# Attention, a channel mix and a routed expert layer in one kernel: how the dispatch builds its index tables, and where three small slots stand

## The chip, the cores and the metric

The kernel runs as one program on one core of a Trainium2 chip. The metric is the time of one execution on the device in microseconds, the median of three runs; lower is better. A profile comes from one further execution. Engines: TensorE (PE), VectorE (DVE), ScalarE (ACT), GpSimd (POOL) and SyncE (SP), which issues most DMAs.

## The reference

Three layers follow one another; batch 4, 576 tokens each, width 512.

```python
# 1: attention, 8 heads of 64, masked by blocks of 64
scores = where(block_i >= block_j, q @ k.T / 8, -1e9); x = softmax(scores) @ v
# 2: a mix of each token with the one before it
xk = mu_k * x + (1 - mu_k) * x_prev;  xr = mu_r * x + (1 - mu_r) * x_prev
x = sigmoid(xr @ w_r) * (relu(xk @ w_k) ** 2 @ w_v)
# 3: each token takes its own best of 8 experts, or the expert of the token before it
fresh = argmax(x @ w_gate);  e = fresh if s == 0 or local_gate[s] < 0.5 else prev_e
out = softmax(x @ w_gate)[e] * (relu(x @ w1[e]) @ w2[e])
```

## The kernel before, in words

The 2304 tokens are 18 tiles of 128 and 9 groups of 256. Attention goes head by head, the mix group by group; products that need precision are made of a high and a low half in a reduced type (a "split"), three matmuls for one. After each group the routing finds the expert of each token, its probability (p_all) and its rank among the tokens of its expert so far (rank_all, `route_group`, L898 to L985).

The expert layer works in slots: one slot holds 128 tokens of one expert. It gathers their rows of y_dram (L1227), loads w1 and w2 of the expert if it is a new one (SyncE, L1256), splits them on ScalarE and VectorE, multiplies twice, scales by the probability and scatters the rows to the output (L1236). 19 main slots run always, six more only if they are needed. Three small slots of at most 32 rows each take the remainders of some experts (`small_slot`, L1326); they keep their weights in four buffers of 256 KB, two of which are the wraw buffers, and load them in four batches one after the other. `BEFORE` (L35) says before which main slots they stand in the program: 10, 13 and 15.

`dispatch` (L1010) makes the tables of the slots: which token is in which place (gidx, sidx) and with which probability (pslot). It runs twice: early after group 6, for the first 14 tiles and the slots 0 to 6, while group 7 and 8 are still mixed; and late after group 8, for all 18 tiles and the other slots. Each time it works out the first place of each expert, from it the place of each token, splits the place into slot (place over 128) and partition (place modulo 128), and turns the list around with TensorE (L1125 to L1133): for each tile a one-hot [128 x 128] of the partition (d_lh), a one-hot of the slot (d_sel) and its product with three values of each token (d_rhs), summed over the tiles into a PSUM bank, pinv, which is copied to d_inv. pinv, the flips of y and the logits of the routing share two banks (`aux`, L776; in the profile they are named s and av).

The order on each engine is written by a planner (`schedule`, L93). It gives each operation a priority by the longest way from it to the end, and all that is not of the rank "ffn" comes ahead of the slots by a large constant (L265 to L267). Then it runs through a model of time: whenever an engine is free, the most urgent operation that is ready by the model is put next. VectorE operations on SBUF and GpSimd's arithmetic are kept apart by it (`turn`). On the chip each engine executes its list in that order and waits at each operation until its inputs are there. Nearly all operations are issued by one line, so the profile calls them L273.

Of the kernel before, what the change touches and what calls it, by code (L numbers as in the profile page):

```python
# [23 lines left out]
NT = T // 128  # L24
GT = 256
# [4 lines left out]
EARLY = -(-(EG * GT - 127 * NE) // 128)  # L30
# [1 line left out]


SMALLS, ROWS = 3, 32
BEFORE = (EARLY + 3, EARLY + 6, EARLY + 8)  # L35
SCALE = 0.125
MASK = -1.0e30

# [5 lines left out]
def f(ap):  # L44
    return ap.bitcast(F32)
# [37 lines left out]

OVER = 65.0

BEGIN = {"pe": 950.0, "act": 1960.0, "dve": 850.0, "pool": 850.0, "sp": 650.0}


# [4 lines left out]
def schedule(ops, until=-1, fill=0.0):  # L93
# [3 lines left out]
    n = len(ops)  # L97
# [20 lines left out]
    while left:  # L118
# [10 lines left out]
        a, b = now[e]  # L129
        if b and turn[other[e]] > t:  # L130

            if not a:
                free[e] = min([turn[other[e]]] + [x[0] for x in soon[e][:1]])
                continue
            i = heapq.heappop(a)[1]
        else:
            i = heapq.heappop(b if b and (not a or b[0] < a[0]) else a)[1]
        start[i] = t
        order.append(i)
        left -= 1  # L140
# [35 lines left out]
class Plan:  # L176
# [87 lines left out]
    def issue(self):  # L264
        ops = self.ops  # L265
        until = next(i for i, o in enumerate(ops) if o[0] == "pe" and o[3][0].tensor.name == self.bank)
        start, order = schedule([(o[0], o[5], o[6], o[8], o[9], o[7][0] != "ffn") for o in ops], until if self.warm else -1, 54.0)  # L267
# [9 lines left out]
def fused_kernel(ctx: ExitStack, tc: tile.TileContext, a, out):  # L277
# [82 lines left out]
    def buffers(where, name, shape=None, dtype=F32, n=1):  # L360
        if name not in rings:
            rings[name] = [0] + [where.tile(shape, dtype, name=f"{name}_{i}") for i in range(n)]
        return rings[name]

    def ring(*args):

        r = buffers(*args)
        r[0] += 1
        return r[1 + (r[0] - 1) % (len(r) - 1)]

    def flat(x):
        return x.rearrange("p a b -> p (a b)")
# [525 lines left out]
    def route_group(g, lg, after):  # L898
# [30 lines left out]
        def to_row():  # L929
            v["pk"] = aux()  # L930
            for j in range(2):
                pe.transpose(v["pk"][0:1, j * 128:j * 128 + 128], v["key"][:, j:j + 1], ident)
            scan = ring(rt, "scan", [1, GT], F32, 1)
# [72 lines left out]
    vals = rt.tile([128, NT, 3], F32, name="vals")  # L1006
    es = rt.tile([1, SLOTS + 1], F32, name="es")
    dve.memset(es[:, 0:1], -1.0)

    def dispatch(early):  # L1010

# [1 line left out]


        st = 0 if early else 1
        nt, j0, n = (EG * 2, 0, EARLY) if early else (NT, EARLY, SLOTS - EARLY)
        m = n if early else n + SMALLS
        gidx_s, sidx_s, pslot_s = of_small()
# [1 line left out]

        def small(name, shape, dt=F32):
            return ring(rt, "d_" + name, shape, dt, 1)

        pc = aux()
        sob = small("sob", [128, NE], BF16)
# [74 lines left out]
        if not early:  # L1100
# [8 lines left out]
        posi = small("posi", [128, 2, NT], I32)[:, :, 0:nt]  # L1109
        dve.tensor_tensor(posi[:, 0, :], posf, rank, op=ALU.add)  # L1110
        dve.tensor_scalar(posi[:, 1, :], posi[:, 0, :], 7, None, op0=ALU.logical_shift_right)
        dve.tensor_scalar(posi[:, 0, :], posi[:, 0, :], 127, None, op0=ALU.bitwise_and)
        pmd = small("pmd", [128, 2, NT])[:, :, 0:nt]
        dve.tensor_copy(pmd, posi)


        ts = slice(0, nt) if early else slice(EG * 2, NT)
        phr = small("phr", [128, NT], F32R)[:, ts]
        dve.tensor_copy(phr, p_all[:, ts])
        dve.tensor_scalar(vals[:, ts, 0], tok[:, ts], 1.0, None, op0=ALU.add)  # L1120
        dve.tensor_copy(vals[:, ts, 1], f(phr))
        dve.tensor_tensor(vals[:, ts, 2], p_all[:, ts], f(phr), op=ALU.subtract)
        w = m + m % 2
        pinv = aux()
        for t in range(nt):  # L1125
# [8 lines left out]
        inv = small("inv", [128, 66])[:, 0:3 * w].rearrange("p (k w) -> p k w", k=3)  # L1134
        dve.tensor_copy(inv, pinv[:, 0:3 * w].rearrange("p (k w) -> p k w", k=3))
        dve.tensor_scalar(sidx[st], inv[:, 0, 0:n], -1.0, None, op0=ALU.add)
        dve.tensor_scalar(gidx[st], inv[:, 0, 0:n], -1.0, 0.0, op0=ALU.add, op1=ALU.max)
        dve.tensor_tensor(pslot[st], inv[:, 1, 0:n], inv[:, 2, 0:n], op=ALU.add)
        if not early:

            dve.tensor_scalar(gidx_s, inv[:, 0, n:m], -1.0, 0.0, op0=ALU.add, op1=ALU.max)
            lh = ring(rt, "d_lh", [128, 128], F32R, 2)
# [3 lines left out]
            pe.matmul(pr[:, 0:3 * SMALLS], f(lh), inv[:, :, n:m], start=True, stop=True)  # L1146
            dve.tensor_scalar(sidx_s, pr[:, 0:SMALLS], 4.0, quarter, op0=ALU.mult, op1=ALU.add)
            dve.tensor_copy(inv[:, 0, 0:SMALLS], pr[:, SMALLS:2 * SMALLS])
            dve.tensor_tensor(pslot_s, inv[:, 0, 0:SMALLS], pr[:, 2 * SMALLS:3 * SMALLS], op=ALU.add)


    def units():
# [287 lines left out]
```

## Time and profile before

| | |
|---|---|
| median of 3 runs | 810.71 us (809.32 to 812.0) |
| the profiled execution | 808.18 us |
| its span, first to last instruction | 806.4 us |
| TensorE busy | 778.0 us, 96% of the span |
| VectorE, ScalarE, GpSimd busy | 609.6, 535.3 and 299.9 us |
| mean granted clock of TensorE | 0.988 of full |
| read from and written to HBM | 131.68 and 9.90 MB |

Times in the views count from the first instruction of the span. The attention and the mix fill the span up to about 524 us, the early dispatch lies at about 477 to 504 us, the late one at 543 to 594 us, and the slots run from 525 us to the end. A busy share is the share of a stretch in which an engine works on an instruction; the durations of neighbours overlap a little, so the distance from start to start is the better price of one operation in a row of such. An idle time names what ended it: "<-DVE d_rhs" means that the engine stood still until VectorE had written d_rhs.

### The profile page before, as it was taken

The page shows a single profiled execution, that of the slowest core. Times are in us where ns is not written, and L with a number is a line of the kernel's source. Part 1 is how long each engine was busy: PE and PEld are TensorE (multiplying, and loading weights), DVE is VectorE, ACT ScalarE, POOL GpSimd, SP SyncE. Part 2 cuts the span into 40 slices and gives each one's busy share as a digit, 9 for nine tenths or more (in the row PEclk, how much of TensorE's full clock was granted, in tenths as well). Part 3 has the DMA queues.
Part 4 walks back from the last instruction along what each step waited for, and adds up shares of the span by engine and source line. Part 5 has one row for each costly group of instructions (what it writes and reads, how often), then busy time and mean ns, then how long its engine had stood idle before and what let it go on. Part 6 is the DMA issues. An engine that isn't in the chain of part 4 may idle for free.

```text
span 806.4 us, 15002 instructions
## 1 busy us (share of the span) xinstructions
PE 778.0 (96%) x5040; PEld 640.3 (79%) x5040; DVE 609.6 (76%) x1346; ACT 535.3 (66%) x1156; POOL 299.9 (37%) x275
## 2 busy tenths in 40 slices
PE   8999999999999999999999997999989999999994
PEld 8665798988888989898998986767867777767773
DVE  6986767775789869576785479699999986866840
ACT  3888566983578946265893525469769977867841
POOL 3343585533656427345452332222121521312200
PEclk9999999999999999999999999899999999999998
DMA  8574312211233202201310005111475287695300
GB/s 216 161 211 153 106 57 82 88 45 35 77 92 99 72 17 83 76 28 37 99 45 14 14 27 209 40 39 40 144 248 197 66 275 268 213 327 187 120 15 23
DMA packets 40466, 87.62 MB, mean 109 GB/s; under 512 B 6540, under 2 KB 10640, under 8 KB 40384
## 3 DMA queue, kind: packets, MB, share of 16 engines
q1 hardware_dynamic: 37152, 76.71, 29.6%
q0 software_dynamic: 3232, 9.90, 3.5%
q8 instruction: 41, 0.67, 0.4%
q14 instruction: 41, 0.34, 0.1%
HBM read 131.68 MB, written 9.90 MB: 176 GB/s over the span
## 4 chain that ended last, share of the span: by engine, by line
PE 67%; issue 11%; DVE 11%; DMA 6%; ACT 2%; POOL 1%; SPq 1%; POOLq 0%; ACTq 0%; DVEq 0%
PE acc L273 38%; PE s L273 12%; PE psT L273 9%; PE av L273 6%; DMA out<-xm,sidx 2%; PE acc L1379 1%; DVE wvl L273 1%; DVE attr L273 1%; DVE xm L273 1%; DMA out<-v,ssum 1%; DVE wrl L273 1%; DMA wraw<-in_w 1%; DMA x<-in_w 1%; ACT attr L273 1%; DVE relu L273 1%
## 5 line engine op out<-in xcount | busy, mean ns | idle before, releaser
L273 DVE TENSOR_REDUCE nm<-s 128x1 f32<-128x576 f32 (+4 forms) x132 | 67.7, 547 | 24.2 <-ACT s L273 22.9
L273 PE MATMUL acc<-xh,wkh 128*128 128x256 f32 x288 | 82.1, 295 | 0.9 <-ACT xh L273 0.6
L273 PE MATMUL acc<-xl,wkh 128*128 128x256 f32 x288 | 82.0, 293 | 0.1
L1236 POOL DMA_INDIRECT out<-xm,sidx x19 | 26.3, 1383 | 147.6 <-ACT xm L273 124.9
L273 PE MATMUL acc<-xh,wkl 128*128 128x256 f32 x288 | 80.7, 289 | 0.0
L273 POOL TENSOR_TENSOR attr<-qk,attr 64x512 fp32r<-64x512 f32 (+1 forms) x48 | 65.7, 1368 | 37.8 <-ACT attr L273 30.3
L273 PE MATMUL av<-attr 128*128 128x256 f32 (+3 forms) x336 | 77.4, 288 | 0.8 <-ACT x L273 0.3
L273 DVE TENSOR_TENSOR attr<-psT,attr 64x256 fp32r<-64x256 f32 (+2 forms) x120 | 63.1, 526 | 17.1 <-ACT attr L273 14.7
L273 POOL TENSOR_TENSOR kkl<-relu,kkh 128x512 fp32r<-128x512 f32 x36 | 47.7, 1329 | 61.9 <-ACT kkh L273 53.6
L273 PE MATMUL s<-attr 128*128 128x288 f32 (+3 forms) x288 | 67.1, 300 | 0.6 <-ACT ea L273 0.6
L273 POOL TENSOR_TENSOR xl<-xm,xh 128x512 fp32r<-128x512 f32 x36 | 46.8, 1301 | 49.7 <-ACT xh L273 45.9
L273 ACT ACTIVATE attr<-psT 64x256 fp32r<-64x256 f32 (+2 forms) x120 | 53.0, 463 | 10.4 <-PE psT L273 9.5
L273 PE MATMUL acc<-attr,wrh 128*128 128x512 f32 x160 | 56.7, 405 | 1.1 <-ACT wrh L273 1.1
L273 ACT ACTIVATE xh<-xm 128x512 fp32r<-128x512 f32 x36 | 22.7, 631 | 52.0 <-DVE xm L273 51.9
L273 PE MATMUL acc<-wvh,kkh 128*128 128x512 f32 x144 | 56.6, 414 | 0.0
L273 PEld LDWEIGHTS acc<-xh,wkh 128*128 128x128 f32 x288 | 53.9, 191 | 2.9 <-ACT xh L273 0.9
L273 PEld LDWEIGHTS av<-attr 128*128 128x128 f32 (+1 forms) x336 | 51.5, 166 | 5.3 <-DVE x L273 0.7
L273 PE MATMUL acc<-wvl,kkh 128*128 128x512 f32 x144 | 55.5, 407 | 0.0
L273 PE MATMUL acc<-wvh,kkl 128*128 128x512 f32 x144 | 55.5, 408 | 0.0
L273 PEld LDWEIGHTS acc<-xl,wkh 128*128 128x128 f32 x288 | 54.2, 191 | 1.1 <-POOL xl L273 0.4
L273 PEld LDWEIGHTS acc<-xh,wkl 128*128 128x128 f32 x288 | 54.1, 191 | 0.4
L273 PE MATMUL psT<-ident,eb 128*128 128x128 f32 (+1 forms) x288 | 54.3, 278 | 0.0
(347 smaller groups left out, 2392.8 us busy)
## 6 DMA issues: line engine op xcount, KB each, us to landing
x<-in_w SPq DMA_DIRECT2D x76, 512.0 KB
eb<-in_w SPq DMA_DIRECT2D x38, 512.0 KB
qk<-in_qk SPq DMA_DIRECT2D x24, 544.0 KB
qk<-in_w SPq DMA_DIRECT2D x19, 512.0 KB
d<-in_w SPq DMA_DIRECT2D x19, 512.0 KB
wraw<-in_w SPq DMA_DIRECT2D x24, 256.0 KB
y_dram<-th SPq DMA_DIRECT2D x18, 256.0 KB
v<-in_v SPq DMA_DIRECT2D x28, 160.0 KB
```

The source lines that it names most:

```text
L273: o[2](*o[3], **o[4])
L1236: plan.add("pool", "scatter", lambda: nc.gpsimd.indirect_dma_start(out=out, out_offset=bass.IndirectOffsetOnAxis(ap=at.bitcast(U32), axis= ...
L1379: plan.warm = lambda: pe.matmul(first[:, 0:128], ones, ones, start=True, stop=True)
```

## The change

- **One-hots from ranks alone.** The first place of each expert is a multiple of 128, apart from what is taken off again, so the place modulo 128 is the rank modulo 128. The one-hot of a tile is made from rank_all as soon as that is known, in bf16, once: 0 to 13 at the early dispatch, 14 to 17 at the late one, which uses the first 14 again. They lie in the two wraw buffers (16 tiles) and in a new tile, hots.
- **Selections of many tiles at once.** One comparison and one product make the right-hand sides of 14 tiles (early) or of 6 tiles (late, three times) instead of one each. The values are bf16 parts now: the token number in two, the probability in three, so five columns in place of three. The right-hand sides are in one buffer, d_rhs, which also lends its space to the row of the routing's scan.
- **Rank of the late dispatch.** Its operations have the rank "late", which is ordered with the slots and no more ahead of them.
- **Places of the small slots.** Before the main slots 9, 12 and 18.
- **Short waits in the order.** Where ScalarE, VectorE or GpSimd would take the next ready operation, the planner looks at the next one to become ready on that engine: if it comes within 300 ns (or half the time of the first, if that is less) and is more urgent by over 2000 ns, the engine is left free until then.

```diff
-BEFORE = (EARLY + 3, EARLY + 6, EARLY + 8)
+BEFORE = (EARLY + 2, EARLY + 5, EARLY + 11)
+FIRM, AHEAD, URGENT = ("act", "dve", "pool"), 300.0, 2000.0
@@ schedule
+        if e in FIRM and soon[e]:
+            r, j = soon[e][0]
+            if r < t + min(AHEAD, 0.5 * ops[mine[0][1]][2]) and prio[j] < mine[0][0] - URGENT:
+                free[e] = r
+                continue
+        i = heapq.heappop(mine)[1]
@@ issue
-        ... o[7][0] != "ffn") ...
+        ... o[7][0] not in ("ffn", "late")) ...
@@ dispatch
+    def hot(t):
+        if t >= 16:
+            return hots[:, t - 16, :]
+        x = buffers(a1, "wraw", [128, 512], F32, 2)[1 + t // 8].bitcast(BF16)
+        return x[:, t % 8 * 128:t % 8 * 128 + 128]
+        if not early:
+            plan.rank = ("late", 0, 0)
+        for t in ((slice(0, 12), slice(12, 14)) if early else (slice(14, 16), slice(16, 18))):
+            ri, rf = (small(x, [128, 12], dt)[:, 0:t.stop - t.start] for x, dt in (("ri", I32), ("rf", F32)))
+            dve.tensor_copy(ri, rank_all[:, t])
+            dve.tensor_scalar(ri, ri, 127, None, op0=ALU.bitwise_and)
+            dve.tensor_copy(rf, ri)
+            for i in range(t.start, t.stop):
+                dve.tensor_scalar(hot(i), iota128, rf[:, i - t.start:i - t.start + 1], None, op0=ALU.is_equal)
-        phr = small("phr", [128, NT], F32R)[:, ts]
-        dve.tensor_copy(phr, p_all[:, ts])
-        dve.tensor_scalar(vals[:, ts, 0], tok[:, ts], 1.0, None, op0=ALU.add)
-        dve.tensor_copy(vals[:, ts, 1], f(phr))
-        dve.tensor_tensor(vals[:, ts, 2], p_all[:, ts], f(phr), op=ALU.subtract)
+        v, x = vals[:, ts, :], f(small("phr", [128, NT], F32R)[:, ts])
+        y = posi[:, 0:v.shape[1]]
+        dve.tensor_scalar(y, tok[:, ts], 1.0, None, op0=ALU.add)
+        for i, mask in enumerate((0x7FFFFFF0, 15)):
+            z = x.bitcast(I32)
+            dve.tensor_scalar(z, y, mask, None, op0=ALU.bitwise_and)
+            dve.tensor_copy(v[:, :, i], z)
+        dve.tensor_copy(v[:, :, 2], p_all[:, ts])
+        dve.tensor_tensor(x, p_all[:, ts], v[:, :, 2], op=ALU.subtract)
+        dve.tensor_copy(v[:, :, 3], x)
+        dve.tensor_tensor(v[:, :, 4], x, v[:, :, 3], op=ALU.subtract)
-        for t in range(nt):
-            lh = ring(rt, "d_lh", [128, 128], F32R, 2)
-            dve.tensor_scalar(lh, iota128, pmd[:, 0, t:t + 1], None, op0=ALU.is_equal)
-            sel = ring(rt, "d_sel", [128, 22], F32, 2)[:, 0:w]
-            dve.tensor_scalar(sel, iota25[:, j0:j0 + w], pmd[:, 1, t:t + 1], None, op0=ALU.is_equal)
-            rhs = ring(rt, "d_rhs", [128, 66], F32R, 3)[:, 0:3 * w].rearrange("p (k w) -> p k w", k=3)
-            dve.tensor_tensor(rhs, sel.unsqueeze(1).to_broadcast([128, 3, w]),
-                              vals[:, t, :].unsqueeze(2).to_broadcast([128, 3, w]), op=ALU.mult)
-            pe.matmul(pinv[:, 0:3 * w], lh, rhs, start=(t == 0), stop=(t == nt - 1))
+        k = nt if early else 6
+        for t0 in range(0, nt, k):
+            t1 = slice(t0, t0 + k)
+            sel = small("sel", [128, 6 * 22], BF16)[:, 0:k * w].rearrange("p (t w) -> p t w", w=w)
+            dve.tensor_tensor(sel, iota25[:, j0:j0 + w].unsqueeze(1).to_broadcast([128, k, w]),
+                              pmd[:, t1].unsqueeze(2).to_broadcast([128, k, w]), op=ALU.is_equal)
+            rhs = small("rhs", [128, 6 * 110], BF16)[:, 0:k * 5 * w].rearrange("p (t i w) -> p t i w", i=5, w=w)
+            dve.tensor_tensor(rhs, sel.unsqueeze(2).to_broadcast([128, k, 5, w]),
+                              vals[:, t1, :].unsqueeze(3).to_broadcast([128, k, 5, w]), op=ALU.mult)
+            for t in range(k):
+                pe.matmul(pinv[:, 0:5 * w], hot(t0 + t), rhs[:, t].rearrange("p i w -> p (i w)"),
+                          start=(t0 + t == 0), stop=(t0 + t == nt - 1))
...
```

What is left out of the diff above: the parts are added up again in d_inv (one add for the token number, two for the probability), the slot alone is worked out from the place, and the last small matmul of the late dispatch, which spreads the places of the small slots, has its left side in hots.

## Rows read from the trace of the kernel before

**Rows 1.** The page: busy us, share of the span, instructions of TensorE, its loads and others.
```profile
PE 778.0 (96%) x5040; PEld 640.3 (79%) x5040; DVE 609.6 (76%) x1346; ACT 535.3 (66%) x1156; POOL 299.9 (37%) x275
```

**Rows 2.** Stretches of 20 us: length; busy PE, PEld, DVE, ACT, POOL; clock, DMA, GB/s.
```profile
500.00:520.00 20.00, 16.74 (x63) 13.65 (x64) 13.52 (x32) 7.58 (x11) 7.03 (x4) 0.74 0.13 42
...
560.00:580.00 20.00, 19.98 (x100) 16.04 (x99) 20.00 (x54) 18.16 (x25) 5.37 (x4) 1.00 0.37 118
...
600.00:620.00 20.00, 17.72 (x85) 13.35 (x83) 17.12 (x18) 17.90 (x23) 5.23 (x4) 1.00 0.77 277
```

**Rows 3.** Stretches of 4 us about the early dispatch, the same columns.
```profile
492.00:496.00 4.00, 2.40 (x11) 1.74 (x10) 3.52 (x15) 2.82 (x4) 0.06 (x1) 1.00 0.94 322
496.00:500.00 4.00, 2.32 (x13) 1.78 (x11) 3.67 (x13) 3.52 (x5) 0.54 (x1) 1.00 1.04 399
500.00:504.00 4.00, 1.42 (x6) 1.29 (x6) 4.00 (x9) 2.44 (x3) 1.38 (x1) 0.59 0.20 73
504.00:508.00 4.00, 3.33 (x13) 2.76 (x12) 3.17 (x7) 1.68 (x3) 3.23 (x1) 0.50 0.01 2
```

**Rows 4.** Timeline, TensorE, 494 to 514 us: start, us, instruction, idle before and releaser.
```profile
494.37 0.50 PE L273 MATMUL acc<-wrh,xh 128*128 128x512 f32 x1 [1.38 <-ACT relu L273]
...
498.74 0.57 PE L273 MATMUL av<-d_rhs,d_lh 128*128 128x24 f32 x2 [0.98 <-DVE d_rhs L273]
501.74 0.68 PE L273 MATMUL av<-d_rhs,d_lh 128*128 128x24 f32 x2 [2.43 <-DVE d_rhs L273]
503.26 1.11 PE L273 MATMUL av<-ident,th 128*128 128x128 f32 x4 [0.84 <-DVE d_inv L273]
505.05 1.88 PE L273 MATMUL s<-wg,relu 128*128 128x9 f32 x8 [0.68 <-ACT relu L273]
506.78 0.77 PE L273 MATMUL acc<-wvh,kkh 128*128 128x512 f32 x1
...
510.76 0.48 PE L273 MATMUL acc<-wrl,xh 128*128 128x512 f32 x1
...
512.95 0.40 PE L273 MATMUL acc<-wvh,kkh 128*128 128x512 f32 x1
513.18 0.39 PE L273 MATMUL acc<-wvl,kkh 128*128 128x512 f32 x1
```

**Rows 5.** Timeline, VectorE, 487 to 504 us.
```profile
487.13 1.20 DVE L273 CAST d_pmd<-d_posi 128x28 f32<-128x28 int32 x1
...
488.93 0.28 DVE L273 TENSOR_SCALAR d_lh<-iota,d_pmd 128x128 fp32r<-128x128 f32 x1
489.12 0.17 DVE L273 TENSOR_TENSOR d_rhs<-d_sel,vals 128x24 fp32r<-128x24 f32 x1
489.22 0.22 DVE L273 TENSOR_SCALAR d_sel<-iota,d_pmd 128x8 f32<-128x8 f32 x1
489.35 0.69 DVE L273 SCALAR_TENSOR_TENSOR relu<-relu 128x512 f32<-128x512 f32 x1
...
503.04 0.17 DVE L273 COPY d_inv<-av 128x24 f32<-128x24 f32 x1
```

**Rows 6.** Timeline, GpSimd, at 487 us.
```profile
487.02 1.27 POOL L273 TENSOR_TENSOR xl<-xm,xh 128x512 fp32r<-128x512 f32 x1
```

**Rows 7.** Timeline, ScalarE, at 504 us.
```profile
504.41 0.59 ACT L273 COPY relu<-av 128x512 f32<-128x512 f32 x1 [1.57 <-DVE gidx L273]
```

**Rows 8.** Timeline, TensorE, 600 to 620 us: after the late dispatch.
```profile
604.18 0.50 PE L273 MATMUL s<-kkh,wrh 128*128 128x512 f32 x1 [2.09 <-ACT xm L273]
...
617.01 0.60 PE L273 MATMUL psT<-ident,ea 128*128 128x128 f32 x4
```

**Rows 9.** Timeline, GpSimd: the gather of slot 7, the third small slot's scatter.
```profile
593.10 1.65 POOL L1227 DMA_INDIRECT ea<-y_dram,gidx  x1 [4.78 <-PE psT L273]
...
767.71 1.01 POOL L1366 DMA_INDIRECT out<-v,ssum  x1 [5.15 <-ACT v L273]
```

**Rows 10.** DMA issues: names, queue, kind, count, median us to landing.
```profile
ea<-y_dram,gidx POOLq DMA_INDIRECT x19, 5.0
```

More of the change, by code (lines that the diff above doesn't have):

```diff
@@ L134, in schedule @@
                 continue
-            i = heapq.heappop(a)[1]
+            mine = a
         else:
-            i = heapq.heappop(b if b and (not a or b[0] < a[0]) else a)[1]
+            mine = b if b and (not a or b[0] < a[0]) else a
+        if e in FIRM and soon[e]:
[4 more added lines that the diff above has]
+        i = heapq.heappop(mine)[1]
         start[i] = t
@@ L266, in issue @@
         until = next(i for i, o in enumerate(ops) if o[0] == "pe" and o[3][0].tensor.name == self.bank)
-        start, order = schedule([(o[0], o[5], o[6], o[8], o[9], o[7][0] != "ffn") for o in ops], until if self.warm else -1, 54.0)
+        start, order = schedule([(o[0], o[5], o[6], o[8], o[9], o[7][0] not in ("ffn", "late")) for o in ops], until if self.warm else -1, 54.0)
         for i in order:
@@ L932, in to_row @@
                 pe.transpose(v["pk"][0:1, j * 128:j * 128 + 128], v["key"][:, j:j + 1], ident)
-            scan = ring(rt, "scan", [1, GT], F32, 1)
+            scan = ring(rt, "d_rhs", [128, 6 * 110], BF16, 1).bitcast(F32)[0:1, 0:GT]
             init = 0.0 if scan_prev[0] is None else carry
@@ L1005, in fused_kernel @@
     taken = rt.tile([128, NE], F32, name="taken")
-    vals = rt.tile([128, NT, 3], F32, name="vals")
+    vals = rt.tile([128, NT, 5], BF16, name="vals")
+    hots = rt.tile([128, 2, 128], BF16, name="hots")
     es = rt.tile([1, SLOTS + 1], F32, name="es")
     dve.memset(es[:, 0:1], -1.0)
+    def hot(t):
[3 more added lines that the diff above has]
+        return x[:, t % 8 * 128:t % 8 * 128 + 128]
     def dispatch(early):
         st = 0 if early else 1
+        if not early:
+            plan.rank = ("late", 0, 0)
         nt, j0, n = (EG * 2, 0, EARLY) if early else (NT, EARLY, SLOTS - EARLY)
@@ L1108, in dispatch @@
             dve.tensor_tensor(posf, posf, far, op=ALU.add)
[L1109 to L1113, printed above, removed]
+        posi = small("posi", [128, NT], I32)[:, 0:nt]
+        dve.tensor_tensor(posi, posf, rank, op=ALU.add)
@@ L1114, in dispatch @@
+        dve.tensor_scalar(posi, posi, 7, None, op0=ALU.logical_shift_right)
+        pmd = small("pmd", [128, NT])[:, 0:nt]
         dve.tensor_copy(pmd, posi)
         ts = slice(0, nt) if early else slice(EG * 2, NT)
-        phr = small("phr", [128, NT], F32R)[:, ts]
-        dve.tensor_copy(phr, p_all[:, ts])
-        dve.tensor_scalar(vals[:, ts, 0], tok[:, ts], 1.0, None, op0=ALU.add)
-        dve.tensor_copy(vals[:, ts, 1], f(phr))
-        dve.tensor_tensor(vals[:, ts, 2], p_all[:, ts], f(phr), op=ALU.subtract)
+        v, x = vals[:, ts, :], f(small("phr", [128, NT], F32R)[:, ts])
@@ L1134, in dispatch @@
-        inv = small("inv", [128, 66])[:, 0:3 * w].rearrange("p (k w) -> p k w", k=3)
-        dve.tensor_copy(inv, pinv[:, 0:3 * w].rearrange("p (k w) -> p k w", k=3))
+        k = nt if early else 6
[10 more added lines that the diff above has]
+                          start=(t0 + t == 0), stop=(t0 + t == nt - 1))
@@ L1136, in dispatch @@
+        inv = small("inv", [128, 110])[:, 0:5 * w].rearrange("p (k w) -> p k w", k=5)
+        dve.tensor_copy(inv, pinv[:, 0:5 * w].rearrange("p (k w) -> p k w", k=5))
+        dve.tensor_tensor(inv[:, 0, :], inv[:, 0, :], inv[:, 1, :], op=ALU.add)
         dve.tensor_scalar(sidx[st], inv[:, 0, 0:n], -1.0, None, op0=ALU.add)
         dve.tensor_scalar(gidx[st], inv[:, 0, 0:n], -1.0, 0.0, op0=ALU.add, op1=ALU.max)
-        dve.tensor_tensor(pslot[st], inv[:, 1, 0:n], inv[:, 2, 0:n], op=ALU.add)
+        dve.tensor_tensor(inv[:, 1, :], inv[:, 2, :], inv[:, 3, :], op=ALU.add)
@@ L1139, in dispatch @@
+        dve.tensor_tensor(inv[:, 1, :], inv[:, 1, :], inv[:, 4, :], op=ALU.add)
+        dve.tensor_copy(pslot[st], inv[:, 1, 0:n])
         if not early:
             dve.tensor_scalar(gidx_s, inv[:, 0, n:m], -1.0, 0.0, op0=ALU.add, op1=ALU.max)
-            lh = ring(rt, "d_lh", [128, 128], F32R, 2)
+            lh = flat(hots).bitcast(F32)
             dve.tensor_copy(lh.rearrange("p (t r) -> p t r", r=ROWS),
@@ L1145, in dispatch @@
             pr = aux()
-            pe.matmul(pr[:, 0:3 * SMALLS], f(lh), inv[:, :, n:m], start=True, stop=True)
+            pe.matmul(pr[:, 0:2 * SMALLS], lh, inv[:, 0:2, n:m], start=True, stop=True)
             dve.tensor_scalar(sidx_s, pr[:, 0:SMALLS], 4.0, quarter, op0=ALU.mult, op1=ALU.add)
-            dve.tensor_copy(inv[:, 0, 0:SMALLS], pr[:, SMALLS:2 * SMALLS])
-            dve.tensor_tensor(pslot_s, inv[:, 0, 0:SMALLS], pr[:, 2 * SMALLS:3 * SMALLS], op=ALU.add)
+            dve.tensor_copy(pslot_s, pr[:, SMALLS:2 * SMALLS])
     def units():
```

## Prediction

> **What bounds the kernel now.** I began with the busy time of each engine: TensorE is busy for 778.0 of the 806.4 us of the span [rows 1]. A change elsewhere shortens the kernel only where TensorE stands still, runs at half clock, or has work taken from it. So the next view was the stretches of 20 us, to find where TensorE is not full: 500 to 520 us has 16.74 busy at a mean granted clock of 0.74, and 600 to 620 us has 17.72 [rows 2]. The first lies at the early dispatch, the second a little behind the late one. In stretches of 4 us the first hole runs from 492 to 508 us, where TensorE is busy 2.40, 2.32, 1.42 and 3.33 us, 9.47 of 16: 6.5 us idle [rows 3].
>
> The timeline of TensorE says what it waited for [rows 4]: 1.38 us for ScalarE's eviction before 494.37, then 0.98 and 2.43 us for d_rhs, 0.84 us for d_inv and 0.68 us for the copy of the transposed y. All but the first are one chain. The sums of the early dispatch stand in the bank av until d_inv is copied at 503.04 [rows 5]; the next flip of y uses the same bank; ScalarE's copy of it sits behind that at 504.41 [rows 7]; the logits at 505.05 read the copy and free the relu buffer that the last eviction of group 8 needs. TensorE executes in its written order, so group 8's last product starts only at 506.78. It starts cold: nine 512-column matmuls take from 506.78 to 510.76, 0.44 us each, where two of them start 0.23 us apart at 512.95 and 513.18 [rows 4]. These are the 1.2 and the 2.4 GHz level; the granted clock fell to 0.59 and 0.50 after the stops [rows 3].
>
> Why the chain is long: VectorE makes a one-hot, a selection and a product for each of 14 tiles. Starts in its timeline are 0.19, 0.13 and 0.10 us apart, 0.42 us a tile and 5.9 us for 14 [rows 5]. From d_pmd at 487.13 to d_inv at 503.04 it takes 15.9 us, because splits of weights of 1.2 us stand between the tiles, and because short operations stretch while GpSimd works: d_pmd takes 1.20 us beside GpSimd's 1.27 us subtraction that began at 487.02 [rows 5, 6].
>
> **The early dispatch.** Removed from the chain: 14 times 0.42, 5.9 us. Added behind d_pmd: the new value columns, one after the other on one scratch tile, nine steps at up to 0.2 us (the distance from d_lh to its reader d_rhs [rows 5]), 1.8 us; one selection of 112 elements, about 0.2 us; one product of 14 x 5 x 8 = 560 elements, for which the nearest row is 0.69 us for 512 elements [rows 5], so 0.75 us; 14 short matmuls back to back, under 1 us; the copy and one more add, 0.3 us. That is 4 us; with one stretched operation (1.1 us) and one split in its way (1.2 us), 6.3 us. d_inv comes at about 488.3 + 6.3 = 494.6 instead of 503.04, before TensorE is through with the twelve products that it began at 494.37 (12 x 0.23 us, so at 497.2).
>
> The product reads both its inputs by broadcast, and the row beside it is a 1x price [rows 5]. The Trainium skill (VectorE: DVE Perf Modes, section "What auto-detection actually checks") says that an operation of two sources reaches double rate only if every tensor is 16-bit with step ±1; bf16 alone would by that earn nothing here. At double rate the product would cost about 0.4 us instead of 0.75 us, at single rate the 0.75 us; the sum does not move by it, since d_inv is early enough either way.
>
> What TensorE gets back: of 6.5 us idle the 1.38 us for the eviction stays (VectorE has no part in it), and I leave 0.7 us for one more short stop, so 4.4 us. The lonely pairs of d_rhs matmuls, 0.57 and 0.68 us counted as busy, go beside other work: 1.0 us. If the clock stays up, the nine matmuls give back 9 x 0.21 = 1.9 us, and the flip and the logits (1.11 and 1.88 us at half clock [rows 4]) half of their time, 1.5 us. Sum: 8.8 us.
>
> Against it, the one-hots move ahead. They need the wraw buffers, which serve the last normalisation first, so twelve of them (0.19 each, 2.3 us) and their preparation (six small operations at 0.1) fall into the time just ahead of d_pmd, in which VectorE also mixes group 8. I take 1.5 us of delay to group 8, between 0 (they fill pauses) and 2.9 us (all of it). Early sum: 8.8 - 1.5 = 7.3 us, bounds 5.9 and 8.8.
>
> Does it last? From 560 to 580 us VectorE is busy 20.00 of 20 and TensorE 19.98 [rows 2], so VectorE must come along. It idles 6.5 us from 500 to 520 [rows 2], and both dispatches take work from it, so I count no loss; if that cover is missing, 3 us.
>
> **The late dispatch.** 18 tiles lose at least 0.42 us each, 7.6 us of a full VectorE. Added: four one-hots and their preparation, 1.4 us; three selections of 132 elements (0.2 to 0.3 each), 0.8; three products of 660 elements, 0.69 x 660/512 = 0.9 each, 2.7; columns and adds, 0.7. Net 2.0 us less. TensorE's hole before 604.18, 2.09 us for the scaled result xm of a slot [rows 8], is the end of a row of late splits, late loads and a late ScalarE. I take 1.5 us of it, between 0 and 2.1. The three products share one buffer, so the second and third wait for TensorE's six matmuls and VectorE's queue stands behind them: up to 0.5 us each, covered as long as the order puts splits between.
>
> **The new rank of the late dispatch** costs nothing by its margin: the gather of slot 7 went at 593.10 [rows 9], takes 1.65 us on GpSimd and about 5.0 us to land [rows 10], and TensorE first transposes its rows at 617.01 [rows 8]: over 17 us to spare.
>
> **Small slots and short waits.** Before slots 9, 12 and 18 instead of 10, 13 and 15: the same work. The third ended with its scatter at 767.71 [rows 9], 39 us before the end of the span, so a move by three slots of 48 products each (11 us at 0.23 us) could use up that margin. The waits of up to 0.3 us in the order change the order everywhere, on engines that TensorE mostly covers. No row shows either; I take 0 for both together, between -3 and +3 us.
>
> **Sum.** 7.3 + 1.5 = 8.8 us off the profiled execution's 808.18 gives 799.4. The median of the runs is 810.71, 2.5 us above the profiled one; off that it is 801.9, and 802 is the forecast.
>
> **Rivals.**
> 1. VectorE and ScalarE take half back. For: VectorE is full at 560 us [rows 2], and ScalarE's order around 494 us has conversions of slot 0's weights in it, each waiting for its load, as the stop of 1.38 us shows [rows 4]. Against: VectorE's 6.5 us of pause at 500. Then half clock (3.4 us) and 1 us remain of it: 4.4 us, 806.3.
> 2. The late dispatch, without its rank, comes too late (the other side). Its some sixty short operations now stand behind splits of 1.2 us on a full VectorE. It decides once the rows of slot 7 are known later than about 8 us before TensorE gets there. Slot 7 would be due near 608, so the table would have to slip from just before 593 to behind 600, and it hurts as far as it slips: at 612 TensorE waits 12 us and loses some 2 us to the clock, and with 8.8 us won the end is 5 us later, 816. The small slots' loads push the same way, since their buffers now hold one-hots until the late sums are done and SyncE's queue stands behind them. Against: 17 us of margin.
> 3. Nothing gained: the one-hots delay group 8 by all 2.9 us, the order with waits costs 3 us and slot 18 waits 2 us for the third small slot: 810.
> 4. More: the small slots relieve the loads and the waits help, +3 and +2 us: 797.
>
> **How the numbers follow.** The forecast (798 to 805) 0.60; rival 1 0.14; rival 2 0.10; rival 3 0.09; rival 4 0.07. About 0.3%, 2.4 us, is what a measurement of this kernel can tell from no change. Faster: 0.60 + 0.14 + 0.07 = 0.81; same 0.09; slower 0.10. The range reaches from 796 (below it half of rival 4, 0.04) to 810 (above it rival 2 and part of rival 3, 0.14).
>
> **What would show it.** Right: TensorE's idle time between 490 and 512 under 3 us with the clock at 1.00; d_inv before 497; group 8's last products done near 515 instead of 524; the hole at 600 gone or under 1 us; the rest shifted as it is. Wrong: the same stop with another name (ScalarE behind a load) at 495 to 503; a hole of TensorE before slot 7 with the gather as its releaser; a last scatter that belongs to a small slot; or a difference that arises before 470 us, which only the short waits could make.

## The result, and the profile after

The changed kernel takes 799.12 us, the median of its runs, beside 811.36 us for the kernel before on the same chip: a ratio of 0.9848 (95% interval 0.9821 to 0.9875). One of its six runs took 1151.52 us at a mean granted clock of 0.608; the ratio leaves it out, and without it the median is 798.18 us. Its profiled execution took 800.11 us, with a span of 798.4 us; against the profiled one of before (span 806.4) that is 8.0 us less. The medians are 12.2 us apart, so some 4 us of the gain can't be found in these two traces.

The page first: TensorE's busy time fell by 7.2 us [rows 1].

```profile
PE 770.8 (97%) x5051; PEld 635.1 (80%) x5051; DVE 605.5 (76%) x1301; ACT 535.6 (67%) x1156; POOL 290.9 (36%) x275
```

The stretches of 20 us, with the columns of [rows 2], and one more at 340 us. That one answers to a row of the kernel before that was not shown; it stands in the second fence.

```profile
340.00:360.00 20.00, 19.63 (x151) 18.62 (x150) 16.34 (x38) 13.49 (x34) 12.98 (x11) 1.00 0.08 29
500.00:520.00 20.00, 19.43 (x103) 15.70 (x103) 16.55 (x42) 13.96 (x17) 2.05 (x1) 0.96 0.19 65
560.00:580.00 20.00, 20.00 (x99) 16.06 (x98) 19.34 (x54) 16.79 (x22) 2.89 (x3) 1.00 0.53 170
600.00:620.00 20.00, 16.76 (x74) 13.43 (x75) 16.85 (x17) 17.64 (x24) 5.09 (x4) 0.91 0.62 232
```

The kernel before, from 340 us:

```profile
340.00:360.00 20.00, 18.82 (x148) 18.29 (x148) 14.62 (x38) 13.22 (x35) 10.14 (x9) 0.91 0.16 55
```

So the hole at 500 is nearly closed, the hole at 600 is still there (16.76 busy instead of 17.72), and TensorE is fuller and faster already at 340 us, far from either dispatch. The 4-us stretches about the early dispatch, as in [rows 3]:

```profile
492.00:496.00 4.00, 3.00 (x13) 2.00 (x11) 3.93 (x5) 1.90 (x3) 2.61 (x3) 1.00 0.95 354
496.00:500.00 4.00, 3.14 (x10) 2.54 (x11) 4.00 (x5) 3.30 (x5) 0.00 (x0) 0.78 1.05 405
500.00:504.00 4.00, 4.00 (x15) 3.19 (x15) 3.25 (x3) 3.18 (x3) 0.00 (x0) 0.79 0.34 126
504.00:508.00 4.00, 4.00 (x20) 3.16 (x19) 2.14 (x3) 2.45 (x3) 0.00 (x0) 1.00 0.00 2
```

TensorE is idle 1.9 of these 16 us, where it was 6.5. Its timeline (as [rows 4]) names the one stop that is left; ScalarE's timeline (as [rows 7]) says where it comes from.

```profile
496.86 0.50 PE L282 MATMUL acc<-wvh,kkh 128*128 128x512 f32 x1 [1.86 <-ACT th L282]
...
498.43 0.63 PE L282 MATMUL acc<-wvh,kkh 128*128 128x512 f32 x1
498.86 0.63 PE L282 MATMUL acc<-wvl,kkh 128*128 128x512 f32 x1
...
501.77 0.62 PE L282 MATMUL acc<-wvl,kkh 128*128 128x512 f32 x2
502.24 0.62 PE L282 MATMUL acc<-wvh,kkl 128*128 128x512 f32 x2
```

```profile
485.80 0.59 ACT L282 COPY relu<-av 128x512 f32<-128x512 f32 x1 [0.55 <-PE av L282]
...
495.27 1.06 ACT L282 ACTIVATE attr<-qk 128x1024 fp32r<-128x1024 f32 x1 [1.47 <-DMA qk<-in_w]
496.23 0.58 ACT L282 ACTIVATE th<-acc 128x512 f32<-128x512 f32 x1
```

ScalarE stood 1.47 us before a conversion whose load had not landed, and the eviction th stands behind it. Behind the stop the clock fell to half for some 3 us: starts are 0.43 us apart at 498.43, and 0.23 us (two matmuls in one row) from 501.77.

VectorE at the early dispatch, as [rows 5]: from d_pmd to d_inv it now takes 5.7 us instead of 15.9. GpSimd, as [rows 6], in the fence behind it.

```profile
478.95 0.17 DVE L282 CAST d_pmd<-d_posi 128x14 f32<-128x14 int32 x1
...
481.64 1.88 DVE L282 TENSOR_TENSOR d_rhs<-d_sel,vals 128x560 bf16<-128x560 bf16 x1
...
484.67 0.20 DVE L282 COPY d_inv<-av 128x40 f32<-128x40 f32 x1
484.91 1.05 DVE L282 TENSOR_TENSOR d_inv<-d_inv 128x8 f32<-128x8 f32 x1
```

```profile
481.63 1.28 POOL L282 TENSOR_TENSOR kkl<-relu,kkh 128x512 fp32r<-128x512 f32 x1 [6.72 <-issue]
```

Behind the late dispatch, TensorE as in [rows 8] and GpSimd as in [rows 9]; the last line is the DMA row of [rows 10].

```profile
602.78 0.50 PE L282 MATMUL s<-wkh,wrh 128*128 128x512 f32 x1 [2.85 <-ACT xm L282]
603.75 0.59 PE L282 MATMUL psT<-ident,ea 128*128 128x128 f32 x3 [0.46 <-DMA ea<-y_dram,gidx]
```

```profile
595.68 1.57 POOL L1266 DMA_INDIRECT ea<-y_dram,gidx  x1 [8.65 <-DVE gidx L282]
...
786.33 0.98 POOL L1405 DMA_INDIRECT out<-v,ssum  x1 [9.20 <-ACT v L282]
789.97 0.98 POOL L1275 DMA_INDIRECT out<-xm,sidx  x1 [2.66 <-DMA out<-v,ssum]
```

```profile
ea<-y_dram,gidx POOLq DMA_INDIRECT x19, 5.3
```

The margin of slot 7's gather is gone: it goes 2.6 us later than before, and TensorE needs its rows 13 us earlier (603.75 for 617.01) and waits 0.46 us for them. At the end, slot 18's scatter waits 2.66 us for the third small slot's.

Where the 8.0 us came and went is read best from milestones of TensorE and ScalarE, here us after the start of the span, from the traces of all kernels that decide something. K8 is the first product of group 8's mix (acc<-xh,wkh), V8 the last start of its acc<-wvh,kkh; S0 to S18 are ScalarE's scaled results xm of the slots.

| kernel | d_inv | K8 | V8 | S0 | S4 | S7 | S18 | span |
|---|---|---|---|---|---|---|---|---|
| before | 503.0 | 478.2 | 522.7 | 546.8 | 603.5 | 640.7 | 795.9 | 806.4 |
| after | 484.7 | 473.1 | 509.6 | 532.6 | 584.6 | 628.5 | 786.4 | 798.4 |
| tables alone | 507.1 | 479.5 | 527.1 | 551.3 | 605.2 | 642.3 | 796.8 | 807.2 |
| tables alone, values ahead | 495.5 | 479.7 | 520.1 | 544.2 | 599.1 | 636.2 | 791.1 | 801.8 |
| waits alone | 488.5 | 473.4 | 514.7 | 537.0 | 599.1 | 638.7 | 795.9 | 806.4 |
| waits and rank | 487.4 | 472.4 | 512.9 | 535.1 | 586.8 | 632.0 | 791.6 | 802.2 |
| after, no waits | 505.2 | 477.1 | 524.7 | 549.8 | 600.2 | 648.0 | 803.1 | 815.3 |
| after, old rank | 488.0 | 476.4 | 511.2 | 549.0 | 599.2 | 636.7 | 791.4 | 803.4 |
| after, old places | 487.6 | 474.6 | 510.1 | 533.2 | 585.3 | 628.1 | 785.2 | 795.7 |
| the same, experts first | 484.7 | 473.1 | 509.7 | 532.9 | 583.8 | 625.1 | 780.4 | 790.7 |

From the first two lines: 5.1 us are won by K8, 7.9 more by V8 and 1.1 by S0; then 2.0 are lost by S7, 2.7 by S18 and 1.5 in the tail, 8.0 in all but for rounding. Between S0 and S7 the gain first rises, from 14.2 us to 18.9 at S4, and then 6.7 us are lost by S7.

### The profile page after: what moved, and what is told of

Same layout as the page of the kernel before. It is cut to its first block, busy times and chain, and to the rows that moved or that the text cites. A ratio compares the mean times of both kernels' runs of the same rounds, so it can differ in the third digit from the quotient of the medians.

```text
span 798.4 us, 14950 instructions
## 1 busy us (share of the span) xinstructions
PE 770.8 (97%) x5051; PEld 635.1 (80%) x5051; DVE 605.5 (76%) x1301; ACT 535.6 (67%) x1156; POOL 290.9 (36%) x275
## 4 chain that ended last, share of the span: by engine, by line
PE 67%; issue 12%; DVE 7%; DMA 6%; ACT 5%; POOL 2%; SPq 0%; POOLq 0%; ACTq 0%
PE acc L282 37%; PE s L282 13%; PE psT L282 8%; PE av L282 6%; PE acc L1418 2%; ACT attr L282 2%; DMA out<-xm,sidx 2%; DMA out<-v,ssum 1%; DMA ea<-y_dram,gidx 1%; DVE xm L282 1%; DMA qk<-in_w 1%; ACT ea L282 1%; DMA wraw<-in_w 1%; DVE attr L282 1%; DMA th<-in_w 1%
## 5 line engine op out<-in xcount | busy, mean ns | idle before, releaser
L1275 POOL DMA_INDIRECT out<-xm,sidx x19 | 22.1, 1162 | 174.9 <-ACT xm L282 172.3
L282 DVE TENSOR_TENSOR attr<-psT,attr 64x256 fp32r<-64x256 f32 (+2 forms) x120 | 63.0, 525 | 15.9 <-ACT attr L282 13.6
L282 PE MATMUL acc<-attr,wrh 128*128 128x512 f32 x160 | 60.2, 409 | 0.0
L282 DVE TENSOR_TENSOR wrl<-psT,wrh 128x512 fp32r<-128x512 f32 x57 | 39.2, 687 | 24.2 <-ACT wrh L282 23.8
```

What stands on the lines that cost most here:

```text
L1275: plan.add("pool", "scatter", lambda: nc.gpsimd.indirect_dma_start(out=out, out_offset=bass.IndirectOffsetOnAxis(ap=at.bitcast(U32), axis= ...
```

## The experiments

My theory after this reading: the tables win the early dispatch, and the short waits win the 5 us ahead of it. The runs were made to try that. Each ratio is to runs of the kernel before on the same chip. Each row of milestones is one trace, and the planner's order shifts everywhere with any edit, so a difference of a few us at one milestone can be order alone: K8 is 1.5 us later with the old places and 3.3 us later with the old rank, though neither edit concerns work ahead of it.

**Without the short waits.**

```
-FIRM, AHEAD, URGENT = ("act", "dve", "pool"), 300.0, 2000.0
+FIRM, AHEAD, URGENT = (), 300.0, 2000.0
```

> The changed kernel without the short waits in the order. In its profile 5.2 us were won before the early dispatch, where only the order differs from the kernel before. If the waits won them and they last, this one is about 5 us slower than the changed kernel, 804, with group 8 starting near 478 us again. Rival: whatever is won before the dispatch is given back in the slots, which are bound by loads and VectorE there; then it is 799 to 800 and only the shape of the slots differs.

The time is 815.72 us, a ratio of 1.0074 (1.0049 to 1.0098): slower than the kernel before, and 12 us more than the theory expected. The early d_inv falls back to 505.2, and the low-ranked late dispatch ends 25 us later than in the changed kernel, as VectorE's timeline shows:

```profile
619.66 0.17 DVE L282 TENSOR_SCALAR gidx<-d_inv 128x18 int32<-128x18 f32 x1
```

S4 is still 3.3 us earlier than before, and S7 is 7.3 us later. That is the place of my second rival and its late table, but not its wait: of TensorE's stops from 600 to 640 us the gather of slot 7 makes 0.79 us, and ScalarE's conversions wrh make 4.2 us in four stops.

**Old places of the small slots.**

```
-BEFORE = (EARLY + 2, EARLY + 5, EARLY + 11)
+BEFORE = (EARLY + 3, EARLY + 6, EARLY + 8)
```

> The changed kernel with the small slots before slots 10, 13 and 15 as before. In the changed kernel's profile the third small slot ended at the very end (785.7 us, its scatter beside the last one) and the tail behind the last matmul is 1.6 us longer. If the new places cost that and no more is behind it: 1 to 3 us faster, 796 to 798. Rival: the new places spread the loads, and without them TensorE waits for pieces from 700 to 760 us as in the kernel before: 2 to 4 us slower, 801 to 803.

The time is 795.00 us, 0.9818 (0.9793 to 0.9842): a little less than the changed kernel, but the intervals overlap. (The last experiment takes it up again.)

**The late dispatch at its old rank.**

```
-        if not early:
-            plan.rank = ("late", 0, 0)
```

> The changed kernel with the late dispatch ahead of the slots again. Theory: the low rank let the list of experts for slots 7 and on be written only at 590 us, SyncE could not start the next loads before 593, ScalarE's queue stood behind them and TensorE lost 2.9 us and some clock before 603. With the old rank the list is out 25 us earlier, that hole closes and the kernel is 2 to 4 us faster, 795 to 797. Rival: the late dispatch ahead of the splits makes a full VectorE late for the slots at 545 to 580 us instead: no gain, 798 to 801.

The time is 803.22 us, 0.992 (0.9897 to 0.9944). The theory fell, and the loss is larger than the rival had it: V8 is at 511.2, but S0 at 549.0, later than before. TensorE's timeline shows the price of a late dispatch that the waits keep together:

```profile
537.88 0.71 PE L282 MATMUL s<-d_rhs,wraw 128*128 128x110 bf16 x6 [7.09 <-DVE d_rhs L282]
```

Behind it the theory's mechanism did come. With the old rank evi is written at 532.5 and TensorE has no hole at 600 us; the same stretch of the changed kernel, in the first line, has 3.2 us of it (columns of [rows 2]). From S4 to S7 the old rank takes 37.4 us, the low rank 43.9. So the low rank wins 16.4 us by S0 and gives 6.5 back from S4 to S7.

```profile
600.00:604.00 4.00, 0.76 (x4) 0.47 (x5) 3.16 (x4) 3.71 (x6) 0.99 (x1) 1.00 1.00 385
...
600.00:604.00 4.00, 4.00 (x21) 3.25 (x20) 2.88 (x3) 4.00 (x6) 2.34 (x2) 1.00 1.06 407
```

**The tables alone.** The kernel before with the new one-hots, selections and value columns; no waits, old rank, old places (the three edits above together).

> The kernel before with the new tables alone (one-hots from the ranks, selections of many tiles at once), old rank, old places, no waits. Group 8 should start at 478 as before, its last products should end 8 us earlier (515), and the end should be 8 to 10 us earlier than before: 801 to 803. Rival: without the other parts the slots give half of it back to a full VectorE: 805 to 807.

The time is 808.07 us, 0.9985 (0.9971 to 1.0): no gain that can be told from none. VectorE's timeline shows why, link by link:

```profile
490.28 0.16 DVE L282 CAST d_pmd<-d_posi 128x14 f32<-128x14 int32 x1
491.61 1.23 DVE L282 TENSOR_TENSOR attr<-eb,attr 128x1024 fp32r<-128x1024 f32 x1 [1.17 <-ACT attr L282]
...
499.50 0.18 DVE L282 CAST vals<-d_phr 128x14 bf16<-128x14 int32 x1
499.58 1.22 DVE L282 TENSOR_TENSOR wkl<-x,wkh 128x1024 fp32r<-128x1024 f32 x1
...
502.02 0.17 DVE L282 TENSOR_TENSOR d_phr<-p_all,vals 128x14 f32<-128x14 f32 x1
502.12 1.22 DVE L282 TENSOR_TENSOR wkl<-x,wkh 128x1024 fp32r<-128x1024 f32 x1
503.25 0.18 DVE L282 CAST vals<-d_phr 128x14 bf16<-128x14 f32 x1
...
505.68 0.73 DVE L282 TENSOR_TENSOR d_rhs<-d_sel,vals 128x560 bf16<-128x560 bf16 x1
507.13 0.20 DVE L282 COPY d_inv<-av 128x40 f32<-128x40 f32 x1 [0.71 <-PE av L282]
```

The value columns use one scratch tile, so nearly each step needs the one before it. In the changed kernel a step takes 0.17 to 0.20 us, and the next one starts some 0.2 us behind its start; here the order fills nearly each of the pauses between them with a 1.2-us split, eight in all, 9.7 us. The rest is the steps themselves, two of which take 1.24 and 1.27 us beside operations of GpSimd, and waiting (1.17 and 1.07 us for ScalarE, 0.71 us for TensorE). From d_pmd to d_inv it takes 16.9 us, no less than the 15.9 of fourteen tiles.

**The waits alone**, on the kernel before:

```
+FIRM, AHEAD, URGENT = ("act", "dve", "pool"), 300.0, 2000.0
...
+        if e in FIRM and soon[e]:
+            r, j = soon[e][0]
+            if r < t + min(AHEAD, 0.5 * ops[mine[0][1]][2]) and prio[j] < mine[0][0] - URGENT:
+                free[e] = r
+                continue
```

> The kernel before with the rule of the short waits and nothing else. Theory (the waits pay twice: some 5 us of order by 473 us, and at the early dispatch only together with the tables, which leave one chain without long steps): the first matmul of group 8 moves from 478.2 to about 473, d_inv from 503.0 to about 498 with the same distance behind d_pmd as before, and the kernel ends 4 to 6 us earlier, 804 to 806. Rival A (the waits alone bring most of what the change brings, also at the dispatch, because they also keep the fourteen tile steps together): 797 to 800, d_inv before 492. Rival B (the 5 us by 473 us need the tables, since the old dispatch's many steps fill the waits): within 2 us of the kernel before.

The time is 809.38 us, 0.9992 (0.9978 to 1.0007). It agrees with rival B, while the early d_inv is the sign of rival A. The milestones show that the waits do much of what I had put down to the tables: K8 is 4.8 us earlier and d_inv 14.5, with the fourteen old tile steps (from d_pmd to d_inv 9.3 us instead of 15.9; 5.7 with the tables as well), and S0 9.8 us. Then all of it is given back before S1: with waits and its old rank, the late dispatch stands in TensorE's way, two short matmuls at a time, and the clock goes to half (stretches of 4 us, TensorE's timeline behind them).

```profile
544.00:548.00 4.00, 2.74 (x11) 1.85 (x9) 4.00 (x26) 0.00 (x0) 0.00 (x0) 0.85 0.63 235
548.00:552.00 4.00, 3.63 (x10) 2.80 (x10) 3.96 (x14) 0.64 (x1) 0.00 (x0) 0.50 0.00 0
```

```profile
546.75 0.75 PE L282 MATMUL s<-d_rhs,d_lh 128*128 128x66 f32 x2 [0.32 <-DVE d_rhs L282]
```

A gain and a loss of 10 us each can look like no effect; only the milestones tell them apart.

**The tables alone, value columns made ahead.** As the tables alone, with the block that fills vals moved up to right behind the tables:

```
+        y = small("posi", [128, NT], I32)[:, 0:v.shape[1]]
...
         pc = aux()
...
-        y = posi[:, 0:v.shape[1]]
```

> The tables without the short waits, without the low rank and with the old places, as in the kernel that came out at 808.07, but the five value columns are made right behind the tables, before the places are known, so that only d_sel, d_rhs and the matmuls stand behind d_pmd. Theory (the gain of the tables was eaten by a 1.2-us split between every two links of a chain of ten): with two or three links left, d_inv comes about 9 us earlier, near 497 to 499, TensorE's stops at 497.7 and 506.5 shrink by 5 to 8 us in all, and the kernel takes 800 to 804. Rival (the time between the links is not lost: the splits that stand there have to be done before group 8 anyway, and VectorE's total work sets the date): d_inv moves, the stops move elsewhere, 806 to 809.

The time is 802.47 us, 0.9906 (0.988 to 0.9931), as the theory had it; d_inv, at 495.5, is a little earlier still. VectorE's timeline has two links behind d_pmd, not ten, and no split between them:

```profile
490.55 0.18 DVE L282 CAST d_pmd<-d_posi 128x14 f32<-128x14 int32 x1
490.75 0.28 DVE L282 TENSOR_TENSOR d_sel<-iota,d_pmd 128x112 bf16<-128x112 f32 x1
...
491.07 0.74 DVE L282 TENSOR_TENSOR d_rhs<-d_sel,vals 128x560 bf16<-128x560 bf16 x1
...
495.45 0.19 DVE L282 COPY d_inv<-av 128x40 f32<-128x40 f32 x1
```

So the chain of value columns, not the tables, kept that version from its gain; waits or a shorter chain each mend it.

**Waits and low rank on the old one-hots**, with the old places: the waits alone, and the three lines of the rank put back.

> The kernel before with the short waits and the low rank of the late dispatch; its old one-hots (one VectorE step of a one-hot, a selection and a product per tile) and old places stay. With the waits alone the early dispatch came out 14.5 us earlier (d_inv 488.5) and slot 0 of the experts' stage 9.8 us, and all of it was lost at 544 to 559, where TensorE waited for the late dispatch's steps. Theory (waits and low rank make the gain, the tables little; the low rank keeps the late steps out of TensorE's way): slots 0 to 3 stay 9 to 11 us earlier, the late chain, longer by some 6 us of VectorE than with the tables, ends at 598 to 605 instead of 595, so slot 7 waits 3 to 8 us for its gather: 799 to 804, against 795.0 for the same kernel with the tables. Rival A (the tables are needed for it: eighteen times three low-ranked steps find no room, the late gidx comes at 615 or later): 808 to 816. Rival B (the tables bring nothing beside waits and rank): 794 to 797.

The time is 805.32 us, 0.9953 (0.9931 to 0.9975), just above the theory's range. By the milestones its mechanism came: S0 and S4 are 11.8 and 16.7 us earlier than before, and then the longer late chain is too late for slot 7, as TensorE's timeline says:

```profile
607.92 0.76 PE L282 MATMUL psT<-ident,ea 128*128 128x128 f32 x4 [4.09 <-DMA ea<-y_dram,gidx]
```

With the tables (the run with the old places) it is 795.0: beside waits and rank the tables are worth some 1.35% (0.9818 to 0.9953). The two traces show less of it than the medians, 10.3 us apart: 2.8 us at V8, 3.9 by S7, 6.4 by S18.

**Experts' numbers first.** The changed kernel with the old places; the late dispatch keeps its old rank from behind its four one-hots up to evi.

```
+        was = plan.rank
         if not early:
             plan.rank = ("late", 0, 0)
...
+        plan.rank = was
         pc = aux()
...
             dve.tensor_copy(evi[st][:, 0, n:m], part)
+            plan.rank = ("late", 0, 0)
```

> The changed kernel with the old places of the small slots, and the part of the late dispatch up to the slots' experts (evi) at the rank that it had before; only the places themselves keep the low rank. Theory (the stop near 597 to 603 and the half clock behind it come from the experts' numbers: they are written at 590.3, the next loads of weights are issued at 593.5, ScalarE waits for them and TensorE for ScalarE): evi is written before 575, the stop of 2 to 3 us goes, and the kernel takes 2 to 4 us less than with the old places alone (795.0): 791 to 793. Rival (the loads wait for buffers that come free at that time, or the stop is the gather's of slot 7): the stop stays, 794 to 796. Other side: the higher rank holds VectorE's splits up around 530 to 560 as the wholly old rank did (7.3 us there): 797 to 802.

The time is 792.38 us, 0.9788 (0.9767 to 0.9809): the lowest of all, within the theory's range. Its interval still meets that of the old places alone (0.9793 to 0.9842), so a gain over those isn't shown. evi is written at 530.4 instead of 589.8 (VectorE's timeline):

```profile
530.39 0.16 DVE L282 CAST evi<-es 1x18 int32<-1x18 f32 x1
```

The mechanism came by half: at 600 to 604 us the granted clock is 1.00 where the kernel with the old places had 0.70, but a stop of 1.50 us remains at 597.4, behind ScalarE.

**The same on the old one-hots.** Waits, low rank behind evi, old places, one-hots of before: in the kernel of waits and rank the low rank begins only behind evi.

> As the kernel with waits and low rank on the old one-hots and old places, with the experts' part of the late dispatch (up to evi) at its old rank. Same but for the tables as the kernel that came out at 792.38. Theory (the tables are worth 3 to 5 us at the early dispatch and the length of the late chain): 796 to 801, V8's last matmul near 513 instead of 509.7. Rival A: the late gidx at 615 or later, over 805. Rival B: 791 to 794.

The time is 805.63 us, 0.9958 (0.994 to 0.9977): outside all but rival A, whose reason is not it (late gidx at 600.5). With the old late chain, early experts' numbers bring nothing. Whether the 13 us to the run above are the tables' alone I did not settle: the order behind 650 us differs too.

**Both mends.** Experts first, and value columns ahead.

> As the kernel with the experts' part first and the old places, and the value columns made ahead as well. Theory: behind the short waits the chain from d_pmd to d_inv shrinks from 5.7 to about 3 us, but at the early dispatch TensorE already stands only 1.9 us, for ScalarE; so d_inv moves and the time by under 2 us. Rival (the chain still holds group 8's splits up, by its own length): 3 to 4 us less than without it.

The time is 793.45 us, 0.9807 (0.9785 to 0.9829): no difference that can be told from none, as expected. But the expected step did not come: from d_pmd (480.70) to d_inv (487.01) it takes 6.3 us, not 3. The product d_rhs takes 1.83 us here, and two more short steps between take 1.25 and 1.23 us. So the chain's length was not changed by this run, and whether it still decides beside the waits stays open.

**Waits on VectorE alone**, on the version with the experts first.

```
-FIRM, AHEAD, URGENT = ("act", "dve", "pool"), 300.0, 2000.0
+FIRM, AHEAD, URGENT = ("dve",), 300.0, 2000.0
```

> The kernel with the experts' part first (792.38), with the short waits on VectorE alone; ScalarE and GpSimd take what is ready. Theory (the waits work by keeping VectorE's chains of short dependent steps from being cut by 1.2-us splits; that is VectorE's order): within 2 us, 791 to 795, d_inv near 485. Rival (the 5 us that the waits bring ahead of 473 us come from ScalarE, whose copies stand ahead of TensorE there): group 8 starts 3 to 5 us later again and the kernel takes 796 to 798.

The time is 803.00 us, 0.9931 (0.9905 to 0.9957): the theory fell, and the rival's sign came, though the time is 5 us above the rival's range too. K8 is at 478.8, where the kernel before has 478.2, and the stretch at 340 us is again slow (clock 0.83, in the columns of [rows 2]):

```profile
340.00:360.00 20.00, 18.83 (x136) 18.49 (x135) 12.74 (x36) 12.45 (x34) 9.76 (x9) 0.83 0.12 42
```

So the gain ahead of the dispatch needs the waits of ScalarE or GpSimd; which of the two was not tried. They bring more behind it: the 5.7 us at K8 are 10.4 at S18.

**New places on the best version.** Experts first, with the places of the change (the second edit reversed).

> The kernel with the experts' part first (0.9788 of before with the old places, 0.9767 to 0.9809), with the new places of the small slots. Theory (the new places cost some 4 us: the third small slot now ends last, and slot 18's scatter, which TensorE has ready at the end, waits 2.7 us more for the small slot's scatter to land; the rest is order inside the experts' stage): third small out behind 775, slot 18's scatter 2 to 4 us behind its own copy of ScalarE, ratio 0.982 to 0.985, 794 to 798. Rival (the 4 us seen between the changed kernel and the one with the old places is a fluke of the order around 600 us, where the late experts' numbers decided; with those early the places are worth nothing): 0.977 to 0.981.

The time is 799.44 us, 0.9871 (0.9847 to 0.9896), beside 0.9788 (0.9767 to 0.9809) with the old places: here the new places cost 0.8%, some 7 us, more than the theory's 4. (On the changed kernel itself they cost 0.3% with intervals that overlap, and with the new places the early experts' numbers bring nothing, 0.9871 beside 0.9848.) Most of it is not the tail: S7, ahead of all three small slots, is 1.1 us earlier than with the old places, S18, behind them, 6.5 us later, and the end 8.5. The waits of TensorE from 620 to 700 us (what waited, for what, us, times, longest) lie at the small slots: 2.4 us are for their weights, and 2.6 us have no releaser in the profile.

```profile
PE s L1361 <- issue: 2.6, 1, 2.6
PE s L1361 <- DMA wraw<-in_w: 1.6, 2, 1.4
PE s L1361 <- DMA th<-in_w: 0.4, 1, 0.4
PE s L1361 <- DMA relu<-in_w: 0.4, 1, 0.4
```

With the old places, TensorE's waits for loads from 600 to the end are these:

```profile
PE av L1361 <- DMA relu<-in_w: 0.7, 1, 0.7
PE av L1361 <- DMA th<-in_w: 0.2, 1, 0.2
```

## Why the prediction was right, and where it was not

The time was right: 802 forecast, 799.1 measured, 12.2 us below the runs of before where 8.8 were summed (8.0 between the two profiled executions). That is in part luck. In the traces 5.1 us were won ahead of the dispatch, where nothing was forecast, and 6.2 us were lost behind S0, where 1.5 us of gain were; the two nearly cancel. Step by step:

1. **Early dispatch, 7.3 us.** K8 to V8 gained 7.9 us, so the size held, but not by the tables: alone they lose 3.1 us from K8 to V8, the waits alone win 3.2, and only both together win 7.9. The step behind the 7.3 us, "with one stretched operation (1.1 us) and one split in its way (1.2 us), 6.3 us", came out at 5.7 us in the changed kernel and at 16.9 with the tables alone: it counted one split where the order put eight, and no wait for ScalarE. I had costed the operations and not the pauses between dependent ones. The waits close these, with either form of the one-hots (5.7 and 9.3 us). The stretched operations were there: d_rhs took 1.88 us beside GpSimd's 1.28, and, behind the copy to d_inv, the add on it took 1.05.

2. **The eviction's stop and the clock.** "Of 6.5 us idle the 1.38 us for the eviction stays" held, as 1.86 us behind a load; the sign that I had called wrong, the same stop with another name, is this one. The clock did not stay up: 0.78 and 0.79 from 496 to 504.

3. **Small slots and short waits, "I take 0 for both together".** This step failed, and the result hung on it. The waits are worth some 18 us in the changed kernel (2.3%: 1.0074 without them, 0.9848 with them; 815.72 and 799.12 us, on two chips). In the traces 4.0 of these arise by K8 (477.1 and 473.1), and at 340 us first, where without them the clock is 0.91 as in the kernel before. The places cost some 7 us on the fastest version, and on the changed kernel 0.3%, which the runs can't tell from nothing.

4. **Late dispatch, 1.5 us gained.** It lost: from S0 to S7 2.0 us went, and 6.7 us from S4 to S7, with a stop of 2.85 us at 602.78 and half clock behind it (0.57 from 604 to 608). I had counted VectorE's work and not when its parts are done. In the changed kernel evi is written at 590.39, and a batch of SyncE's loads of a slot's weights follows from 593.54. The hole is the low rank's: with the old rank S4 to S7 takes 6.5 us less. An early evi alone, with the new places, takes 2.6 us less; which other late result makes the rest stays open.

5. **The new rank costs nothing by its margin.** By the gather, as I had it, it costs 0.46 us at 603.75, though the 17 us to spare were used up; by the hole of step 4 it costs 6.5 us from S4 to S7. And it is a condition of the gain all the same: with the waits and without the low rank, TensorE stands 7.09 us (d_rhs) and the dispatch's gain is gone by S0. Rival 2 came near in the kernel without waits, where the late table slipped to 619.66. That its 815.7 us meet the 816 of the rival is luck: the early gain that the rival counts on was not there, and the gather held TensorE only 0.79 us.

Of the signs named, d_inv before 497, the idle time under 3 us and the early end of group 8 came (V8 at 509.6, for which 515 was forecast). The clock and the hole at 600 did not. Of those against me, the load behind ScalarE, the gather as releaser, a small slot's scatter just ahead of the last one, and the difference before 470 us all came.

## What to carry to other kernels

A chain of short dependent operations costs not its sum but, where an order is filled greedily, up to one long operation for each pause between links: shorten the chain, make its inputs ahead, or let the engine wait for the next link. A dispatch that is kept together in this way stands in the way of what runs beside it, so what is not yet needed has to get a low rank at the same time. Whether what feeds loads (the experts' numbers) is better taken out of that again is not shown: 0.3% at the best, with intervals that overlap, and nothing in two other versions. Parts of a change that each measure as nothing (the tables alone, the waits alone) can be worth 1.5% together with the rest; the low rank alone and the places alone were not run. The milestones along the span show the gain and the loss that a single time hides.

## What the runs showed of the hardware

A short VectorE operation stretched where GpSimd's had begun just ahead of it. The product d_rhs of 128x560 took 1.88 us in the changed kernel, where GpSimd's subtraction of 1.28 us began 0.01 us ahead of it. It took 0.73 us with the tables alone, where GpSimd had no operation from 502 to 508 us. In the run with the values ahead it was the other way round: d_rhs began 0.10 us ahead of GpSimd's subtraction and took 0.74 us, while the subtraction took 1.79 us and the short step behind d_rhs 1.26 us. So the operation that began second was the one that took longer.

The 0.73 us is near the single rate that the prediction took (0.75 us, from 0.69 us for 512 elements). The Trainium skill (VectorE: DVE Perf Modes, section "What auto-detection actually checks") gives an operation of two sources the double rate only where every tensor is 16-bit with step ±1. In this product vals is repeated along the last dimension, which is step 0, so by that page it runs at the single rate, and the trace agrees.

The granted clock fell from the 2.4 to the 1.2 GHz level between 498 and 499 us (0.63 in that us, 0.50 in the next two), with TensorE busy since 496.86, where its stop of 1.86 us had ended, and rose again between 501 and 502 us (0.67, then 1.00), with TensorE still busy. Not every such stop was followed by it: behind the 1.50 us at 597.4 with the experts' numbers first the clock stayed at 1.00.
